# Shifted copies of v made by on-chip DMAs instead of engine copies, in a gated linear attention with a cosine-gated feed-forward layer

## The chip, the core and the metric

One core of one Trainium2 chip runs the whole kernel. The core has a matrix engine (PE in the profile; PEld is its weight load), a vector engine (DVE), an activation engine (ACT), GpSimd (POOL) and a queue engine (SP) that mostly issues DMAs. The metric is the device time of one execution in microseconds (us); lower is better.

## The reference, cut to what matters

```python
f = 1.0 / (1.0 + np.exp(-f_logit))              # q, k, v, f_logit: [4, 8, 768, 48]
for t in range(S):
    state = f[:, :, t, :, None] * state + np.einsum('bhd,bhe->bhde', k[:, :, t], v[:, :, t])
    y[:, :, t] = np.einsum('bhd,bhde->bhe', q[:, :, t], state)
x = y.transpose(0, 2, 1, 3).reshape(3072, 384)  # 8 heads of 48 channels side by side
h = x @ w_in                                    # [3072, 2048]
g = h * np.cos(h)
return (g @ w_out).astype(np.float32)           # [3072, 384]
```

The first part is a linear attention whose 48 x 48 state of each head decays by a gate per channel. It is computed in chunks of 128 tokens: within a chunk by masked scores, between chunks by the state. The second part is a feed-forward layer over all 3072 tokens.

## The kernel before

**Tiling.** The 3072 tokens are 12 pairs of two chunks (three pairs for each of four batch entries). `pair(n)` does the attention for one pair of 256 tokens: it loads f, k, q and v with DMAs (`f{n}`, `k{n}`, ...; pairs 0 and 1 in two halves, `f0.0`, `f0.1`), makes the decays on ACT (`ex`, `ln`, `fx`, then `eb` and `ei` from the cumulated sums `cum` on PE), the decayed q and k (`qa`, `ka`, `qm`, `km` on DVE or POOL), turns those two round (`tq`, `tk` on PE and a copy `qkt`, or for pairs 4 to 11 a DMA transpose `tq` issued on SP), makes the scores (`sc` on PE), masks them (`am` on DVE), carries the state (`ps` on PE, `st` and `sz` on DVE and POOL) and sums the output in PSUM: `y{n}` from masked scores and v, `yi{n}` from the state. `xe{n}.0` and `xe{n}.1` copy it to SBUF as bf16. Of v there is a bf16 cast `vb{n}` and then `vt{n}`, which is the operand that PE loads as weights for `y`.

**The feed-forward part.** `moe(m, ...)` works on units of 128, 128 and then eleven times 256 tokens. `h{m}.js` is the first product (each step 0.65 us of PE in the timeline, 12 matmuls on 128 tokens or 6 on 256), `co` the cosine on ACT, `g` the product on DVE, `o{r}.s` the second product (4 matmuls a step, 0.65 us), `ot` its copy to SBUF and `out` its store. The weights come in eight loads `w0.i` (w_in) and `w1.i` (w_out), each cast to bf16 by `wc`.

**What `vt` is for.** PE writes the output of a head in blocks of 32 of the 384 channels. A head has 48, so blocks 3i and 3i+2 belong to one head and block 3i+1 to two. In the kernel before, `vt` has for each chunk and head 80 columns: 16 zeros, the 48 of v, 16 zeros. `blocks(h)` picks 32 columns at 16 and 48 (even head) or 0 and 32 (odd head), so the shared block gets its half from each head and zeros from the other. Four copies `vt{n}.0` to `vt{n}.3` (64 partitions x 384 each) fill it from `vb`, moving rows between partition halves where the token order asks for it.

**Order.** A string `ORDER` lists every step by hand: its name, its engine (T is PE, S ACT, V DVE, G POOL, Y SP) and the buffer that each new value takes. `emit` issues the steps in this order, so it is the order of each engine's queue; semaphores between the engines follow from what a step reads and writes. A DMA issued on SP waits, on SP, for the data that it reads and for its buffer to be free, and it waits too until the DMA that used its semaphore lane before, eight DMAs earlier, has landed. Steps behind it on the queue wait with it. The steps `zf` are matmuls on zeros at the start.

Of the kernel before, what the change touches and what calls it, by code (L numbers as in the profile page):

```python
# [15 lines left out]
B, H, S, D = 4, 8, 768, 48  # L16
# [13 lines left out]
SLOTS = {"f": 3, "k": 3, "q": 3, "v": 3, "sp": 3, "ls": 2, "b": 3, "bi": 3, "qk": 3, "vb": 3, "vt": 3, "qkt": 5, "am": 4,  # L30
         "sz": 4, "st": 2, "x": 4, "g": 5, "co": 4, "ot": 4}
WITHIN = 12
ZEROS = 38
# [3 lines left out]
f0.0:Y0 f0.1:Y q0.0:S0 f1.1:S1 k0.0:S0 f1.0:Y ex0.0:S q0.1:Y k0.1:Y zsp.0:V zvt.2:V ln0.0:S0 zf0:T0  # L37
zf1:T0 zf2:T0 zf3:T0 zf4:T0 zf5:T0 zf6:T0 zf7:T0 zf8:T0 cum0.0:T0 fx0.0:S ei0.0:S0 ex0.1:S eb0.0:S0
ln0.1:S v0:Y0 ex1.1:S qa0.0:V zqk.2:V ka0.0:G zqk.1:G qm0.0:V2 km0.0:V fx0.1:S qa0.1:V zf9:T1
zf10:T1 zf11:T1 zf12:T1 zf13:T1 zf14:T1 zf15:T1 zf16:T1 tq0.0:T0 cum0.1:T1 ka0.1:G k1.0:Y1 q1.0:Y1  # L40
f2:Y2 k1.1:Y zf17:T2 tk0.0:T ei0.1:S ex1.0:S ln1.0:S0 eb0.1:S qkt0.0:V0 qm0.1:V km0.1:G vb0:V0
zsz.3:G zvt.0:G vt0.1:G2 zsz.2:G zf18:T2 zf19:T2 cum1.0:T2 sc0.0:T0 eb1.0:S1 ln1.1:S tq0.1:T3
cum1.1:T4 tk0.1:T ei1.1:S0 fx1.0:S qkt0.1:S1 am0.0:V0 ka1.0:G zsz.0:V qa1.0:V qm1.0:G1 ei1.0:S
ps0.1:T5,6 ps0.0:T sz0.01:V0 sz0.00:V vt0.0:V km1.0:V q1.1:Y v1:Y1 f3:Y0 vt0.2:S eb1.1:S fx1.1:S
ex2:S ln2:S0 vt0.3:S ka1.1:G zf20:T7 zf21:T7 zf22:T7 zf23:T7 zf24:T7 zf25:T7 zf26:T7 zf27:T7 yi0:T7
tq1.0:T5 tk1.0:T sc0.1:T2 km1.1:G qkt1.0:S1 st0.11:V0 sz0.11:V2 zsz.1:V qa1.1:V st0.10:V am0.1:V1
sz0.10:V vb1:S0 w0.1:Y0 zf28:T0 zf29:T0 zf30:T0 zf31:T0 tk1.1:T6 sc1.0:T4 y0:T2 ex3:S xe0.1:S0
qm1.1:G ln3:S1 am1.0:V2 ad2:G0 tq1.1:T ps1.1:T3,0 ps1.0:T cum2:T1 w0.0:Y1 qkt1.1:V0 st1.00:V0
vt1.2:V2 st1.01:V zf32:T4 sc1.1:T4 ad3:V0 zf33:T6 zf34:T6 zf35:T6 zf36:T6 zf37:T6 cum3:T3 sz1.00:G0
vt1.0:G sz1.01:G vt1.3:G wc0.1:S ei2:S0 ei3:S1 eb2:S0 eb3:S2 w0.2:Y2 am1.1:V0 yi1:T7,6 xe0.0:V  # L50
vt1.1:V w0.3:Y3 h1.01:T4 y1:T st1.10:V0 st1.11:V xe1.0:V1 xe1.1:V h0.01:T0 fx3:S wc0.2:V wc0.0:G
h0.00:T h1.00:T co0.0:S0 co1.0:S1 h2.00:T6 h2.01:T h2.10:T2 h2.11:T g0.0:V2 g1.0:V1 h2.21:T0 h2.20:T
wc0.3:G zsp.1:G co2.0:S2 co2.1:S0 co2.2:S1 h1.10:T4 h1.11:T q3:Y0 w1.0:Y4 k3:Y1 w1.1:Y0 co1.1:S3
g2.0:V3 qa3:V g2.2:V g2.1:V g1.1:V wc1.0:G h0.11:T6 h0.10:T h2.31:T0 qm3.1:V1 co0.1:S1 g0.1:V
h2.30:T ka3:G km3.1:G sz1.10:G0 km3.0:G qm3.0:G wc1.1:S co2.3:S3 g2.3:V sz1.11:V o0.0:T2 q2:Y1
w1.2:Y4 k2:Y0 fx2:S qa2:V ka2:V qm2.1:V2 o1.0:T3 o3.0:T4 o0.1:T o2.0:T5 tk3.0:T6 tq3.0:T tk3.1:T7
o1.1:T tq3.1:T o2.1:T qkt3.0:S0 o3.1:T sc3.0:T0 qkt3.1:S1 w1.3:Y0 v2:Y1 sc3.1:T6 am3.0:V0 wc1.2:G
qm2.0:G km2.0:G km2.1:G o2.2:T o3.2:T am3.1:V2 f4:S2 tq2.0:T0 tk2.1:T1 tq2.1:T wc1.3:G v3:Y0 vb2:S0
qkt2.1:V2 o0.2:T tk2.0:T vt2.0:V2 vt2.1:S ex4:S qkt2.0:V3 ps2.0:T1 ps2.1:T sc2.1:T6 am2.1:V1
st2.01:V0 st2.00:V ln4:S1 o2.3:T o1.2:T o3.3:T sc2.0:T6 vt2.2:G fx4:S ad4:V1 vb3:G1 sz2.00:G2  # L60
vt3.2:V0 ps3.0:T1,0 ps3.1:T f5:Y0 k4:Y0 ot3:S0 ex5:S ln5:S1 o1.3:T cum4:T4 o0.3:T ei4:S0 ot0:S1
ot2:S2 vt3.0:G vt3.1:G sz2.01:G vt2.3:G ka4:G am2.0:V3 vt3.3:V yi2:T6,7 y2:T ot1:V3 sz3.01:V1
sz3.00:V v4:Y1 ad5:V1 xe2.0:V1 q4:Y1 y3:T1,3 yi3:T km4.0:G1 vb4:G1 xe2.1:S eb4:S0 xe3.0:S0 k5:Y1
cum5:T2 v5:Y0 q5:Y0 km4.1:V st3.10:V0 st3.11:V eb5:S1 fx5:S ei5:S0 sz3.11:G1 zsp.2:G sz3.10:V
xe3.1:V h3.11:T6 h3.20:T4 ps4.0:T0,1 ps4.1:T st4.00:V0 st4.01:V qa4:V sz4.00:G0 sz4.01:G st4.10:V0
st4.11:V h3.10:T co3.1:S3 h3.21:T h3.00:T2 h3.01:T co3.2:S1 co3.0:S0 ka5:G km5.1:G2 vb5:G0 qm4.1:G
qm4.0:G zqk.0:G km5.0:G vt4.2:G0 h4.10:T0 h4.11:T g3.1:V2 f7:Y1 f6:Y2 out1:Y co4.1:S3 tq4.1:Y0
# [119 lines left out]
def describe(nc, cpool, ppool, q, k, v, f_logit, moe_w_in, moe_w_out, out):  # L187
    G = Graph()
# [53 lines left out]
    vbS = slots("vb", [128, 2, H, D])  # L242
# [453 lines left out]
```

## Time and profile before

| | before |
|---|---|
| median of 3 runs | 189.81 us (189.21 to 189.86) |
| the profiled execution, its own time | 191.71 us |
| its span, first to last instruction | 189.9 us |
| granted PE clock, mean | 0.980 |
| busy: PE, PEld, DVE, ACT, POOL | 173.3, 124.1, 152.3, 128.5, 95.0 us |
| DMA packets, bytes | 74106, 34.45 MB |
| copies `vt<-vb`: POOL, DVE, ACT | 24 of 552 ns, 12 of 543 ns, 12 of 507 ns (means) |

The profiled execution took 1.8 us more than its span, and 1.9 us more than the median of the runs. A busy PE in the profile is not PE at its peak, since matmuls are pipelined; the number of matmuls by their spacing says more than the busy share. Busy shares over the whole span mix stages: the start up to 25 us, in which little but loading and the first two pairs goes on; a middle up to 150 us, in which pairs and feed-forward units alternate; and a tail in which PE alone works off the second products.

### The profile page before, as it was taken

The page shows a single profiled execution, that of the slowest core. Times are in us where ns is not written, and L with a number is a line of the kernel's source. Part 1 is how long each engine was busy: PE and PEld are TensorE (multiplying, and loading weights), DVE is VectorE, ACT ScalarE, POOL GpSimd, SP SyncE. Part 2 cuts the span into 40 slices and gives each one's busy share as a digit, 9 for nine tenths or more (in the row PEclk, how much of TensorE's full clock was granted, in tenths as well). Part 3 has the DMA queues.
Part 4 walks back from the last instruction along what each step waited for, and adds up shares of the span by engine and source line. Part 5 has one row for each costly group of instructions (what it writes and reads, how often), then busy time and mean ns, then how long its engine had stood idle before and what let it go on. Part 6 is the DMA issues. An engine that isn't in the chain of part 4 may idle for free.

```text
span 189.9 us, 5936 instructions
## 1 busy us (share of the span) xinstructions
PE 173.3 (91%) x2510; PEld 124.1 (65%) x2512; DVE 152.3 (80%) x212; ACT 128.5 (68%) x180; POOL 95.0 (50%) x126
## 2 busy tenths in 40 slices
PE   7779779999979969999999999996989999999992
PEld 2354469855658834778657777665858887666651
DVE  4498999999998998699999899799999898502040
ACT  3959859895579993778795889986634877212321
POOL 2287576838698997446254896499921000000000
PEclk9979999999999996999999999999999999999999
DMA  6999999959996579899799998994790000004043
GB/s 149 261 261 306 387 343 326 289 174 273 265 256 145 147 160 210 194 276 197 195 206 283 268 242 145 232 244 101 102 155 3 3 0 0 3 0 166 0 166 124
DMA packets 74106, 34.45 MB, mean 181 GB/s; under 512 B 67424, under 2 KB 72544, under 8 KB 74080
## 3 DMA queue, kind: packets, MB, share of 16 engines
q1 hardware_dynamic: 70416, 32.71, 72.9%
q10 hardware_dynamic: 3664, 1.38, 3.2%
q8 instruction: 19, 0.31, 0.7%
q14 instruction: 7, 0.06, 0.1%
HBM read 25.17 MB, written 4.72 MB: 157 GB/s over the span
## 4 chain that ended last, share of the span: by engine, by line
PE 35%; DVE 24%; DMA 17%; POOL 7%; ACT 6%; issue 5%; SPq 3%; ACTq 1%; POOLq 0%; DVEq 0%
PE ps L585 18%; DVE g L551 11%; PE ps L569 11%; DMA k<-in_k_dram 7%; DMA v<-in_v_dram 6%; DVE am L448 3%; DVE q L336 3%; POOL qk L394 3%; DMA qkt<-qk 2%; DVE qk L394 2%; DMA out_dram<-ot 2%; PE ps L521 2%; POOL k L344 1%; PE ps L444 1%; SPq L413 1%
## 5 line engine op out<-in xcount | busy, mean ns | idle before, releaser
L574 ACT ACTIVATE co<-ps,halfpi 128x1024 bf16<-128x1024 f32 x48 | 52.0, 1113 | 26.4 <-PE ps L569 25.2
L569 PE MATMUL ps<-x,w_in_bf 128*128 128x256 bf16 (+1 forms) x624 | 67.1, 265 | 2.5 <-DVE g L551 0.9
L585 PE MATMUL ps<-w_out_bf,g 128*128 128x384 bf16 x384 | 69.3, 332 | 0.0
L551 DVE TENSOR_TENSOR g<-ps,co 128x1024 bf16<-128x1024 f32 x48 | 60.1, 1305 | 8.9 <-ACT co L574 8.7
L569 PEld LDWEIGHTS <-w_in_bf 128*128 128x128 bf16 x624 | 56.5, 98 | 11.4 <-issue 3.0
L585 PEld LDWEIGHTS <-g 128*128 128x128 bf16 x384 | 36.5, 99 | 23.0 <-issue 1.3
L448 DVE TENSOR_TENSOR am<-ps,pmask 128x1024 bf16<-128x1024 f32 x24 | 28.8, 1215 | 1.6 <-PE ps L444 1.4
L394 POOL TENSOR_TENSOR qk<-k,bi 128x384 bf16<-128x384 f32 x20 | 21.2, 1068 | 4.2 <-issue 3.3
L493 POOL TENSOR_TENSOR sz<-st,b 64x192 bf16<-64x192 f32 x23 | 13.4, 583 | 17.9 <-DVE st L487 17.0
L394 POOL TENSOR_TENSOR qk<-q,b 128x384 bf16<-128x384 f32 x15 | 15.6, 1049 | 8.2 <-DVE q L336 8.2
L344 POOL TENSOR_TENSOR k<-k,f 128x384 f32<-128x384 f32 (+1 forms) x12 | 11.1, 926 | 7.5 <-DMA k<-in_k_dram 6.3
L195 POOL COPY vt<-vb 64x384 bf16<-64x384 bf16 x24 | 13.2, 552 | 2.0 <-POOL qk L394 0.6
L263 PE MATMUL ps<-zero 128*128 128x512 bf16 x36 | 11.4, 456 | 1.9 <-DVE zero L201 1.2
L195 DVE COPY ot<-ps 128x384 f32<-128x384 f32 x8 | 4.4, 552 | 10.5 <-PE ps L585 10.5
L328 ACT ACTIVATE f<-f 128x768 f32<-128x768 f32 (+1 forms) x14 | 10.4, 746 | 3.6 <-DMA f<-in_f_logit_dram 3.5
L487 DVE TENSOR_TENSOR st<-ps,sz 64x192 f32<-64x192 f32 x32 | 11.2, 352 | 1.6 <-PE ps L521 0.6
L195 ACT COPY ot<-ps 128x384 f32<-128x384 f32 x16 | 7.3, 476 | 6.9 <-PE ps L585 4.8
L444 PE MATMUL ps<-qkt 48*64 48x128 bf16 x384 | 9.0, 220 | 2.8 <-DVE g L551 2.0
L195 ACT CAST x<-ps 128x384 bf16<-128x384 f32 x14 | 6.4, 479 | 6.9 <-DVE x L195 5.1
L336 DVE SCALAR_TENSOR_TENSOR q<-f,q 128x384 f32<-128x384 f32 (+1 forms) x14 | 9.2, 656 | 1.4 <-ACT f L328 1.2
L394 DVE TENSOR_TENSOR qk<-q,b 128x384 bf16<-128x384 f32 x9 | 9.0, 999 | 1.4 <-ACT b L381 1.4
L444 PEld LDWEIGHTS <-qkt 48*64 48x64 bf16 x384 | 6.3, 106 | 5.8 <-issue 3.1
(68 smaller groups left out, 176.3 us busy)
## 6 DMA issues: line engine op xcount, KB each, us to landing
out_dram<-ot SPq DMA_DIRECT2D x24, 192.0 KB, 2.2
v<-in_v_dram SPq DMA_DIRECT2D x11, 384.0 KB, 5.8
q<-in_q_dram SPq DMA_DIRECT2D x10, 384.0 KB, 6.5
k<-in_k_dram SPq DMA_DIRECT2D x10, 384.0 KB, 6.2
f<-in_f_logit_dram SPq DMA_DIRECT2D x9, 384.0 KB, 5.7
g<-in_moe_w_in_dram SPq DMA_DIRECT2D x4, 768.0 KB, 9.3
g<-in_moe_w_out_dram SPq DMA_DIRECT2D x4, 768.0 KB, 7.5
f<-in_f_logit_dram SPq DMA_DIRECT2D x3, 192.0 KB, 4.3
```

The source lines that it names most:

```text
L195: (nc.scalar.copy if e == "ACT" else eng(e).tensor_copy)(out=o, in_=i)
L263: G.step(f"zf{i}", ("PE",), lambda e, dump=dump: nc.tensor.matmul(dump.ap, lhsT=zero[:, 0:128], rhs=zero, start=True, stop=True), writes=[ ...
L336: eng(e).scalar_tensor_tensor(out=w.ap[:, :, 0, :], in0=t.ap[:, :, 1, :], scalar=1.0, in1=w.ap[:, :, 0, :], op0=ALU.add, op1=ALU.mult)
L344: eng(e).tensor_mul(out=w.ap[:, :, 0, :], in0=w.ap[:, :, 0, :], in1=t.ap[:, :, 0, :])
L394: G.step(f"{nm}{n}.{u}", ("POOL", "DVE"), lambda e, u=u, j=j, src=src, dec=dec: eng(e).tensor_mul(out=qkp[u][j].ap[:, :, :, 0:D], in0=swap ...
L444: nc.tensor.matmul(o[t, r, 2 * a + g, :].rearrange("p (e n) -> p e n", e=2), lhsT=qkv(u)[s, 1, a, g, x, :], rhs=qkv(u)[s, 0, a, g, :, :], ...
L448: G.step(f"am{n}.{u}", ("DVE",), lambda e, u=u, sc=sc: nc.vector.tensor_mul(out=am[u].ap.rearrange("p r b n -> p (r b) n"), in0=sc.ap.rear ...
L493: eng(e).tensor_mul(out=new.ap[s, :, r, :].rearrange("p (u a) n -> p u a n", u=2), in0=ap()[s].rearrange("p (u a) n -> p u a n", u=2), in1 ...
L551: nc.vector.tensor_mul(out=o.rearrange("p b (n e) -> p b e n", e=2), in0=ph.ap.rearrange("p (b e n) -> p b e n", e=2, n=64), in1=co.ap.rea ...
L569: nc.tensor.matmul(ph.ap[:, i * T:(i + 1) * T].rearrange("p (g t) -> p g t", t=C), lhsT=w_in_bf[:, kk, f0:f0 + 128], rhs=xa[:, :, kk, :], ...
L574: G.step(f"co{m}.{j}", ("ACT",), lambda e, ph=ph, co=co: nc.scalar.activation(out=co.ap, in_=ph.ap, func=AF.Sin, bias=halfpi), reads=[ph], ...
L585: nc.tensor.matmul(po.ap[:, 0:DM], lhsT=gT.ap[:, j, i * C:(i + 1) * C], rhs=w_out_bf[:, j, :], start=(po.first and j == 4 * s), stop=(po.f ...
```

## The change

The 16 zero columns at each side of `vt` go away: `vt` is now [128, 2, 8, 48] without gaps. The four copies of a pair become four DMAs issued on SP, each of 64 partitions x 768 bytes inside SBUF. A new small tile `vz` holds for each pair of heads 64 columns: the last 16 channels of the even head, 32 zeros, the first 16 of the odd head. One copy of 128 x 256 elements a pair makes it, from `vt`, on DVE, POOL or ACT (2, 6 and 4 of the 12). The shared blocks of `y` read `vz`, the others `vt`. `y{n}` now waits for the four DMAs and for `vz{n}`.

```diff
-SLOTS = {... "vb": 3, "vt": 3, "qkt": 5, ...}
+SLOTS = {... "vb": 3, "vt": 3, "vz": 3, "qkt": 5, ...}
-ZEROS = 38
+ZEROS = 47
...
-    vtS = slots("vt", [128, 2 * H, D + 32], zero=edges)
+    vtS = slots("vt", [128, 2, H, D])
+    vzS = slots("vz", [128, 2, H // 2, 64], zero=lambda t: t[:, :, :, 16:48])
...
         for j, (x, g) in enumerate(((0, 0), (1, 1), (0, 1), (1, 0))):
-            G.step(f"vt{n}.{j}", ("DVE", "POOL", "ACT"), lambda e, x=x, g=g: copy(
-                e, vt.ap[64 * x:64 * x + 64, H * g:H * g + H, 16:16 + D], vb.ap[64 * g:64 * g + 64, x]),
-                reads=[vb], writes=[vtp[j]])
+            G.step(f"vt{n}.{j}", ("SP",), lambda e, x=x, g=g: nc.sync.dma_start(
+                out=vt.ap[64 * x:64 * x + 64, g].rearrange("p h d -> p (h d)"),
+                in_=vb.ap[64 * g:64 * g + 64, x].rearrange("p h d -> p (h d)")), reads=[vb], writes=[vtp[j]])
+        G.step(f"vz{n}", ("DVE", "POOL", "ACT"), lambda e: copy(
+            e, vz.ap.rearrange("p g i (s d) -> p (g i) s d", d=16)[:, :, 0:4:3, :],
+            vt.ap.rearrange("p g (i r) d -> p (g i) (r d)", r=2)[:, :, 32:64].rearrange("p a (s d) -> p a s d", d=16)),
+            reads=[vt], writes=[vz])
...
-            return ((3 * i, 16), (3 * i + 1, 48)) if j == 0 else ((3 * i + 1, 0), (3 * i + 2, 32))
+            return ((3 * i, 0, False), (3 * i + 1, 0, True)) if j == 0 else ((3 * i + 1, 32, True), (3 * i + 2, 16, False))
...
-                   lambda g, b, h, at: dict(lhsT=vt.ap[:, H * g + h, at:at + 32],
-                                            rhs=am[h // 4].ap[:, h % 2, h % 4 // 2 * 2 + g, :]))
+                   lambda g, b, h, at, z: dict(
+                       lhsT=vz.ap[:, g, h // 2, at:at + 32] if z else vt.ap[:, g, h, at:at + 32],
+                       rhs=am[h // 4].ap[:, h % 2, h % 4 // 2 * 2 + g, :]))
...
-        G.step(f"y{n}", ("PE",), inner, reads=[am[0], am[1], vt], writes=py, sums=True)
+        G.step(f"y{n}", ("PE",), inner, reads=[am[0], am[1], vt, vz], writes=py, sums=True)
```

`ORDER` is a new list throughout, with other engines for some steps. Counted over the list: DVE loses 12 `vt`, 2 `qm`, 1 `km`, 1 `vb`, 3 `ad` and 2 `xe` and gains 2 `vz` and 1 `ot`; ACT loses 12 `vt`, 1 `wc` and 1 `ot` and gains 4 `vz`, 2 `xe` and 1 `qkt`, and issues 6 loads where it issued 5; POOL loses 24 `vt` and gains 6 `vz`, 3 `ad`, 2 `qm`, 1 `km`, 1 `vb` and 1 `wc`. SP issues 144 DMAs where it issued 96. ACT still changes between its two tables ten times. Nine more zero matmuls stand at the start.

The head of SP's and ACT's queues, which set the start (buffer numbers left out):

```
SP before:  f0.0 f0.1 f1.0 q0.1 k0.1 v0 k1.0 q1.0 f2 k1.1 q1.1 v1 f3 w0.1 w0.0 w0.2 w0.3 q3 w1.0 k3 ...
SP after:   f0.1 f1.0 q0.0 k0.1 f1.1 k0.0 q0.1 v0 q1.1 k1.1 q1.0 f3 k1.0 vt0.2 vt0.1 vt0.0 k3 vt0.3
            vt1.3 vt1.2 f2 vt1.0 w0.3 vt1.1 w0.2 w0.0 w0.1 w1.3 w1.2 q2 k2 w1.0 v2 v3 w1.1 f5 vt2.3 f4 vt3.0 vt2.0 vt2.1 ...
ACT after:  f0.0 ex0.0 ln0.0 ex0.1 ex1.0 fx0.0 ln0.1 fx0.1 ei0.1 eb0.0 ln1.0 ex1.1 ei0.0 ln1.1 eb0.1 fx1.1 eb1.1 eb1.0
            qkt0.0 ei1.0 ei1.1 fx1.0 v1 ex3 ln3 q3 vb1 fx3 qkt1.1 eb3 ei3 qkt1.0 vz0 ex2 ln2 xe0.1 vz1 ...
PE before its first h1.01: all of pairs 0 and 1 but y1 (it stands one place later), cum2, cum3
PE after before its first h0.11: all of pairs 0 and 1, cum2, cum3, tk3.x, tq3.x, sc3.1
```

More of the change, by code (lines that the diff above doesn't have):

```diff
@@ L38 @@
[L38 to L49, printed above, removed]
@@ L56 @@
[L56 to L67, printed above, removed]
@@ new lines @@
+zf0:T0 zf1:T0 zf2:T0 zf3:T0 zf4:T0 zf5:T0 zf6:T0 zf7:T0 zf8:T0 cum0.0:T0 fx0.1:S k0.1:Y0 f1.1:Y
+k0.0:Y q0.1:Y zf9:T1 zf10:T1 zf11:T1 zf12:T1 zf13:T1 cum0.1:T1 qa0.0:V ka0.0:V zqk.0:G zsz.0:G
+ei0.1:S0 eb0.0:S0 ln1.0:S1 ka0.1:G zsp.0:G km0.1:G1 ex1.1:S ei0.0:S ln1.1:S km0.0:G zsz.2:G eb0.1:S
+fx1.1:S qm0.0:V qa0.1:V qm0.1:V v0:Y0 q1.1:Y1 k1.1:Y1 zf14:T2 zf15:T2 zf16:T2 zf17:T2 zf18:T2
+cum1.0:T2 zf19:T3 zf20:T3 zf21:T3 cum1.1:T3 tk0.1:T1 zf22:T4 tk0.0:T0 tq0.0:T vb0:G0 zf23:T4 zf24:T4
+zf25:T4 zf26:T4 ps0.0:T4,5 tq0.1:T ps0.1:T eb1.1:S1 eb1.0:S qkt0.0:S0 ei1.0:S0 ei1.1:S fx1.0:S
@@ new lines @@
+ka1.1:V qa1.1:V q1.0:Y f3:Y2 k1.0:Y zvz.2:V sz0.01:V2 qa1.0:V v1:S0 km1.1:G1 ex3:S qm1.0:G ka1.0:G
+km1.0:G zsp.2:V sz0.00:V qm1.1:V qkt0.1:V1 ln3:S0 sc0.0:T2 zf27:T6 zf28:T6 zf29:T6 zf30:T6 zf31:T6
+tk1.1:T0 zf32:T6 zf33:T6 zf34:T6 zf35:T6 zf36:T6 zf37:T6 zf38:T6 sc0.1:T6 yi0:T1 tq1.0:T4 st0.11:V0
+st0.10:V vt0.2:Y0 vt0.1:Y vt0.0:Y k3:Y0 q3:S1 vt0.3:Y am0.1:V0 ad3:G2 vb1:S1 fx3:S sz0.10:G2 zf39:T5
+tk1.0:T tq1.1:T ka3:G ps1.1:T5,6 ps1.0:T cum3:T7 qkt1.1:S0 eb3:S2 ei3:S0 qkt1.0:S1 sz0.11:V
+st1.00:V0 st1.01:V am0.0:V1 sc1.1:T2 qa3:V vz0:S2 km3.1:G1 qm3.0:G km3.0:G sc1.0:T4 vt1.3:Y1 vt1.2:Y
@@ new lines @@
+f2:Y1 ex2:S am1.1:V2 qm3.1:V am1.0:V3 y0:T7 tk3.1:T0 sz1.00:G0 sz1.01:G tq3.0:T2 zf40:T3 zf41:T3
+zf42:T3 tk3.0:T tq3.1:T qkt3.1:V2 zf43:T3 zf44:T3 yi1:T3,4 ln2:S0 xe0.1:S0 vt1.0:Y w0.3:Y0 vt1.1:Y
+vz1:S2 zf45:T5 zf46:T5 y1:T sc3.1:T0 qkt3.0:S0 xe0.0:S st1.10:V0 ad2:V2 st1.11:V cum2:T5 wc0.3:G
+ei2:S0 eb2:S0 fx2:S xe1.0:V1 sz1.10:V0 xe1.1:V w0.2:Y1 w0.0:Y2 h0.11:T6 h1.11:T2 wc0.2:G h2.30:T4
+am3.1:V2 w0.1:Y3 h1.10:T co1.1:S0 wc0.0:V g1.1:V2 w1.3:Y4 h2.31:T h0.10:T h2.21:T0 h2.20:T wc0.1:G
+sz1.11:G co0.1:S1 wc1.3:G h2.01:T2 h2.00:T g0.1:V1 h2.11:T6 h2.10:T co2.2:S0 g2.2:V3 w1.2:Y0 q2:Y1
@@ new lines @@
+k2:Y0 h0.01:T0 h0.00:T co2.3:S2 co2.0:S1 w1.0:Y4 v2:Y0 wc1.2:G v3:Y1 co2.1:S0 g2.3:V g2.0:V zvz.0:V
+g2.1:V ka2:G qa2:V qm2.0:G0 qm2.1:G h1.00:T4 h1.01:T co1.0:S1 co0.0:S0 o2.3:T2 o2.2:T o1.3:T3
+o0.2:T6 o3.3:T7 o0.3:T o1.2:T wc1.0:S w1.1:Y0 km2.0:G zsz.3:V g0.0:V km2.1:V g1.0:V tq2.1:T0 o2.0:T
+tk2.1:T vb2:S1 ps2.0:T1 ps2.1:T vb3:G0 tk2.0:T4 tq2.0:T o0.0:T o1.0:T st2.00:V0 st2.01:V qkt2.1:V1
+qkt2.0:S3 ps3.1:T4,5 ps3.0:T sc2.0:T0 sz3.00:V3 am2.0:V3 sz3.01:V f5:Y2 sz2.00:G2 wc1.1:G st3.10:V1
+st3.11:V vt2.3:Y1 o3.0:T o3.2:T f4:Y1 o3.1:T ex5:S o1.1:T ln5:S0 sc3.0:T4 sc2.1:T0 ot1:V0 ad5:G2
@@ new lines @@
+sz2.01:G am3.0:V0 am2.1:V1 vt3.0:Y0 vt2.0:Y vt2.1:Y vt2.2:Y vt3.2:Y k4:Y0 ex4:S o0.1:T o2.1:T
+cum5:T3 yi2:T4,5 ln4:S1 ot0:S1 vz2:S0 fx4:S ad4:G1 eb5:S0 ei5:S0 cum4:T6 ei4:S1 y2:T ka4:G km4.1:G1
+vt3.3:Y vt3.1:Y vz3:V2 ot3:V2 v4:Y1 xe2.0:V0 vb4:G0 f7:Y0 y3:T3,0 yi3:T km4.0:V ot2:V3 sz3.10:V3
+xe3.1:V1 xe2.1:S eb4:S1 fx5:S xe3.0:S ex7:S h3.01:T4 h3.10:T6 ps4.1:T2,3 ps4.0:T h3.00:T sz3.11:G
+st4.00:V1 st4.01:V sz4.00:G0 h3.20:T0 h3.11:T h3.21:T co3.0:S1 q4:Y1 co3.1:S0 sz4.01:G qa4:V
+st4.11:V1 st4.10:V k5:Y1 out3:Y vt4.2:Y0 q5:Y0 qm4.0:G qm4.1:G ka5:G km5.1:G0 km5.0:G out0:Y vt4.1:Y
@@ L526, in inner @@
         def inner(e):
[L527 to L529 removed]
+            summed([(g, b, h, at, z) for g in range(2) for h in range(H) for b, at, z in blocks(h)],
+                   lambda g, b, h, at, z: dict(
+                       lhsT=vz.ap[:, g, h // 2, at:at + 32] if z else vt.ap[:, g, h, at:at + 32],
+                       rhs=am[h // 4].ap[:, h % 2, h % 4 // 2 * 2 + g, :]))
         def inter(e):
```

109 lines of the change are left out of this document (51 added, 58 removed).

## The prediction

> **What bounds the kernel now.** I read the page first (busy time, slices), then the table by stage, the waits of PE in the middle, and the timeline round the longest of them.
>
> ```profile
> PE 173.3 (91%) x2510; PEld 124.1 (65%) x2512; DVE 152.3 (80%) x212; ACT 128.5 (68%) x180; POOL 95.0 (50%) x126
> PE   7779779999979969999999999996989999999992
> DVE  4498999999998998699999899799999898502040
> PEclk9979999999999996999999999999999999999999
> ```
>
> PE and DVE stand at nine tenths together up to slice 32; then DVE runs out and PE goes on alone to the end. The granted clock is below full in two slices only: the third, and the sixteenth (71 to 76 us).
>
> ```profile
> 30.00:60.00 30.00, 28.09 (x468) 20.82 (x466) 29.08 (x40) 23.08 (x30) 21.52 (x25) 1.00 1.05 256
> 60.00:90.00 30.00, 28.01 (x411) 21.05 (x409) 27.26 (x34) 23.82 (x32) 21.44 (x28) 0.94 0.93 187
> 90.00:120.00 30.00, 29.07 (x454) 21.14 (x453) 27.69 (x34) 24.98 (x33) 18.31 (x23) 1.00 1.00 222
> 120.00:150.00 30.00, 27.64 (x540) 20.79 (x539) 28.35 (x41) 20.17 (x31) 17.33 (x23) 1.00 0.60 124
> ```
>
> The columns are the stretch, its length, busy time of PE, PEld, DVE, ACT and POOL, clock, DMA share, GB/s. From 30 to 150 us PE stands idle for 1.9 + 2.0 + 0.9 + 2.4 = 7.2 us, and DVE is busy for 112.4 of 120. So PE is the bound, and DVE, nearly as full, sets most of what PE still loses:
>
> ```profile
> PE ps L444 <- DVE g L551: 2.0, 1, 2.0
> PE ps L521 <- DVE am L448: 1.4, 1, 1.4
> ```
>
> ```profile
> 68.44 1.72 DVE L195 COPY vt<-vb 64x384 bf16<-64x384 bf16 x1
> 70.20 2.51 DVE L551 TENSOR_TENSOR g<-ps,co 128x1024 bf16<-128x1024 f32 x2
> 71.56 0.42 PE L444 MATMUL ps<-qkt 48*64 48x128 bf16 x16 [1.99 <-DVE g L551]
> 71.91 4.34 PE L585 MATMUL ps<-w_out_bf,g 128*128 128x384 bf16 x16
> ```
>
> One `vt` copy on DVE took 1.72 us at 68.44 (the median of these is 0.256). Behind it `g` came late, PE stood for 1.99 us, and its next 16 second-product matmuls took 4.34 us where 16 took 2.76 at 66.46 us, in the slice with the low clock. That one copy is the visible head of a loss of 2.0 + 1.6 = 3.6 us.
>
> **The change part by part.** What goes:
>
> ```profile
> L195 POOL COPY vt<-vb x24: 493/502/847, 12.3 to 142.8; 64x384 bf16<-64x384 bf16 x24
> L195 ACT COPY vt<-vb x12: 495/508/512, 14.2 to 145.1; 64x384 bf16<-64x384 bf16 x12
> L195 DVE COPY vt<-vb x12: 241/256/1724, 14.4 to 122.7; 64x384 bf16<-64x384 bf16 x12
> ```
>
> That is 13.2 us of POOL, 6.1 of ACT and 6.5 of DVE. The `vz` copies put back 128 x 256 elements each; no row is that, and between 0.26 (the `vt` median on DVE) and 0.55 (a `vt` on POOL) I take 0.5 on POOL, 0.3 elsewhere: 3.0, 1.2 and 0.6 us. With the steps that change engine, at the row means, DVE falls by about 12 us in all (6.5 - 0.6 of v; 2 `qm` 2.0, `km` 0.7, `vb` 0.7, 3 `ad` 1.9, 2 `xe` 1.1; `ot` +0.6), ACT by 4, POOL by 2. PE's work stays, but for nine zero matmuls that fill waits of the start.
>
> *The start* (before: first h at 25.22 us). In the new order PE may begin with h only behind `cum2`, so behind f2, and f2 stands on SP behind two `vt1` copies, which wait for `vb1`. On ACT: f0 lands at 4.16 as now; up to `v1` stand eight steps `ex` and `ln` of 0.52, four `fx` of 0.36, eight `ei` and `eb` of 0.33 and `qkt0.0`, 1.01: 13.4. v1 lands 4.6 later (the row of v on ACT's queue), 18.0; `vb1` 0.83: 18.85. Two copies at 0.4 each on SP, then f2 at 19.65 (landing 5.7): 25.35. `ex2`, `ln2` 0.83 + 0.84, `ad2` 0.63, `cum2` 0.56: first h at 28.2, so 3.0 later. By then PE has done 1.6 us more of other work (`y1`, pair 3's four transposes and one score step: 7.8 us against 6.2 at the spacing of the timeline). Net **+1.4 us**; with f2 landing in 3.4 (the shortest of a load) it is -0.9, with the weights late it is +5.0 (a rival below).
>
> *Pairs 2 and 3* (before: 41.4 to 56.8 us). PE had 11 o steps (7.2 us) and attention steps of 5.5 to do in 15.4 us and lost 2.7. In the new order pair 3's transposes and one score are already made, so only pair 2 is still to be turned. Against that, `vt2.0` to `vt2.2` stand on SP behind `vt3.0`, and so behind `vb3` on POOL. I take half of the loss back: **-1.3**, between 0 and -2.7.
>
> *The middle.* Nine of the twelve DVE copies stand after 30 us, 4.6 us of them, with the one of 1.72 among them. Without it the stall at 69.6 goes: **-3.6**. What comes late next is am (1.4 us of PE once), which I leave, since the room that DVE gains may go to any wait: 0, at best -1.2.
>
> *What the DMAs cost.* SP issues 48 more.
>
> ```profile
> out_dram<-ot SPq DMA_DIRECT2D x24, 192.0 KB, 2.2
> v<-in_v_dram SPq DMA_DIRECT2D x11, 384.0 KB, 5.8
> qkt<-qk SPq DMA_TRANSPOSE x16, 3.4
> L592 SPq DMA_DIRECT2D out_dram<-ot x24: 332/450/1473, 60.6 to 187.1; - x24
> ```
>
> The last column of the first three is issue to landing in us; the last row has the time that an issue holds SP, in ns. A copy of 48 KB in 64 rows is nearest to the store: 0.33 to 0.53, I take 0.4, and it lands in about 2.2 us on an empty queue, up to 5.8 behind a load. From 60.1 to 122.4 us SP issues 44 DMAs for 46.35 us and is free for 15.95; 24 copies (pairs 4 to 9) add 9.6, so 56 of 62. In the packets, 48 x 64 = 3072 more are 4% of 74106. `vb` to `y` grows from one engine copy to issue, landing and `vz`: 0.4 x 4 + 2.2 + 0.5 = 4.3 us at the least. From pair 4 on a run of h or o steps of that length lies between in PE's order. Cover is thin where SP is held by a producer: I take three waits of PE of 0.5 us (the wait for `DMA qkt<-qk` of the profile), **+1.5**; ends 0 and 6.4 (rival).
>
> Sum: 1.4 - 1.3 - 3.6 + 1.5 = -2.0; the span goes from 189.9 to 187.9. The profiled execution (191.71 in all) would be 189.7; the runs' median lies 0.1 below its span, so **187.8 us**.
>
> **The rivals.** *SP becomes the bound.* Each `vt` waits on SP for `vb`, and loads, stores and transposes stand behind it. If SP's free 15.95 us are waits for producers that stay, the 9.6 us make it late from 60 us on. For: at 101.47 a load of v was issued whose landing (4.77 us) is in the chain that ended last, so there was no lead; transposes hold SP for 1.2 to 2.7 us each. Against: other loads lie long before their use. It decides once SP is later than the lead of the loads. With two thirds of 9.6 reaching PE, 6.4 in place of 1.5: **192.7**. Slower.
>
> *The copies land one behind another.* Four landings of 2.2 in a row are 8.8 us, 5.0 more than the 3.8 above (four issues and one landing). It would show where the plan has least cover, at pairs 2 and 3, whose copies stand together on SP while PE has only o steps left, and decide if those run out first: 5.0 on top, **192.8**. Slower. For: DMA share is 1.0 or more in most stretches to 120 us. Against: stores queued closely in the tail do not add up so. The Trainium skill ("DMA: Bandwidth & Descriptors", Rules for kernel authors) speaks against the change here: it says to coalesce small transfers, since under 64 KB one pays mostly overhead, and that two transfers to halves of the partitions serialize. By its fit of about 2.0 us + bytes / 436 GB/s a copy would be an estimated 2.1 us, near the row of the store.
>
> *The weights come late.* `w0.3` is issued at 21 here (the first w_in load before: 13.36). If it takes the median of 9.3, it lands at 30.3; the cast, 1.46, lets h begin at 31.8, 3.6 after my sum: **191.4**. Slower. Against: the 9.3 is of four queued together.
>
> *Nothing gained.* DVE's 12 us are off the path, the stall comes back under another name at another place (again with a lowered clock), and the rest of the sum stays: 189.8 + 1.4 - 1.3 = **189.9**, no change.
>
> **How the numbers follow.** No change means within 0.5% (0.95 us), about what a measurement of this kernel can tell. The forecast has 0.46, all faster; nothing gained 0.13; SP 0.20, landing 0.10, weights 0.11, together 0.41 slower. The forecast's own range is 184.0 (f2 early, pairs 2 and 3 without loss, no new wait gives 189.8 - 0.9 - 2.7 - 3.6 = 182.6, not all at once) to 188.8. The range of 8 in 10 reaches up over the rivals to 194.0, since the SP case may be larger than its two thirds.
>
> **What would show it.** Right: no wait of PE over 1.5 us between 30 and 150 us, full clock there, DVE's busy time near 140 us, first h near 28 us, `vt` landing in 2 to 4 us. Wrong: PE or DVE waiting for `DMA vt<-vb` or for `vz`; SP issuing without a gap from 60 to 125 us, with POOL and ACT waiting for loads of k, q and v; the first h after 30 us.

## The result and the profile after

The changed kernel took 197.9 us (median of 196.9, 197.9 and 198.3), the kernel before beside it 189.8: a ratio of 1.040 (from all runs kept, not from the two medians), interval 1.030 to 1.050. It is slower; the forecast was 187.8 with a range up to 194.0. Here and below, medians and ratios leave out runs more than 1.5% above the fastest of their kernel, as one of the change at a clock of 0.57 and 292 us. SP issues 144 DMAs in the new order; in the old one it was 97, one more than stated above.

The page of the profiled execution after the change (197.9 us in all, span 196.1): busy time by engine, two engines by slices, the granted clock by slices.

```profile
PE 176.2 (90%) x2521; PEld 125.7 (64%) x2521; DVE 143.0 (73%) x193; ACT 123.6 (63%) x173; POOL 92.1 (47%) x116
PE   7899499999959998998896999997999799999991
DVE  5399987997966996897993599787999589721020
PEclk9999889999999999999996999999999999999999
```

DVE lost 9 us of work (12 were costed), ACT 5 and POOL 3, and DVE now has slices of 3, 5 and 6 in the middle. PE did not get shorter for it. After the start there is again one slice with a low clock, now the twenty-second (103 to 108 us) instead of the sixteenth.

The table by stage (stretch, length, busy time of PE, PEld, DVE, ACT, POOL, clock, DMA share, GB/s):

```profile
30.00:60.00 30.00, 27.25 (x431) 20.70 (x429) 24.98 (x32) 22.26 (x29) 19.25 (x19) 1.00 1.04 280
60.00:90.00 30.00, 28.88 (x436) 23.01 (x434) 24.31 (x30) 25.53 (x32) 20.63 (x26) 1.00 1.10 221
90.00:120.00 30.00, 26.45 (x396) 19.24 (x395) 23.96 (x32) 20.71 (x28) 15.18 (x19) 0.94 0.95 199
120.00:150.00 30.00, 28.38 (x540) 19.82 (x539) 25.43 (x34) 19.90 (x31) 17.69 (x24) 1.00 0.89 188
```

PE is idle for 9.0 us of these 120, against 7.2 before. The stretch from 90 to 120 lost 2.6 us of busy time, more than the stretch from 60 to 90 gained. DVE has over 4.5 us free in every stretch, though PE still waited twice for its `g` (below).

The longest waits, first of PE, then of the other engines for what the change added (total, times, longest, in us):

```profile
PE ps L449 <- DMA qkt<-qk: 2.1, 1, 2.1
PE ps L591 <- DVE g L557: 2.0, 2, 1.1
PE ps L449 <- DVE am L453: 1.9, 1, 1.9
PE ps L526 <- POOL vz L196: 1.7, 2, 1.3
PE ps L526 <- DMA vt<-vb: 0.7, 1, 0.7
PE ps L526 <- DVE vz L196: 0.7, 1, 0.7
```

```profile
POOL vz L196 <- DMA vt<-vb: 10.9, 3, 6.4
DVE vz L196 <- DMA vt<-vb: 1.8, 1, 1.8
```

The first wait is for a transpose, not for a copy; the one for `am` lies in the start, at 19.6 us; three are for the copies and their tails (`vz`), 3.1 us together, 1.3 of them behind the middle, at 152 us; and POOL stood 10.9 us with `vz` at its head, with everything behind it in its order standing too. The timeline round the first wait (start, length, engine, step; idle before it in brackets):

```profile
94.14 2.93 SPq L418 DMA_TRANSPOSE qkt<-qk  x2
97.13 0.57 SPq L598 DMA_DIRECT2D out_dram<-ot  x1
97.76 1.11 SPq L404 DMA_DIRECT2D vt<-vb  x2
98.92 1.32 SPq L418 DMA_TRANSPOSE qkt<-qk  x1
104.61 0.50 PE L449 MATMUL ps<-qkt 48*64 48x128 bf16 x16 [2.10 <-DMA qkt<-qk]
105.05 1.46 PE L591 MATMUL ps<-w_out_bf,g 128*128 128x384 bf16 x4
```

SP issues the third transpose behind a store and two copies, though its data were ready on POOL at about 92.7. It lands 5.65 us after its issue at 98.92, and PE has run dry. The next four second-product matmuls take 1.46 us where four took 0.81 at 101.70; the granted clock from 100 to 110 us is 0.83. Before, the stall of 1.99 had the same tail: 0.83 from 69.5 to 79.5 us. The page's rows for the DMAs and the rows of the new steps (ns: shortest, median, longest; first and last start in us):

```profile
vt<-vb SPq DMA_DIRECT2D x48, 48.0 KB, 3.5
L404 SPq DMA_DIRECT2D vt<-vb x48: 462/588/2152, 12.1 to 151.0; - x48
DMA to landing us min/median/max: 1.8/3.5/6.4
L196 POOL COPY vz<-vt x6: 388/400/403, 70.5 to 153.1; 128x256 bf16<-128x256 bf16 x6
```

By place: the first h starts at 29.31 (before 25.22), the h of unit 3 at 58.97 (56.80), the last matmul ends at 191.8 (186.6), and after it come 4.3 us (3.3). The two spans differ by 6.2 us; the medians of the runs by 8.1, since the profiled execution of before was 1.9 above its own median.

### The profile page after: what moved, and what is told of

The parts are those of the page before. It is cut to its first block, busy times and chain, and to the rows that moved or that the text cites. A ratio compares the mean times of both kernels' runs of the same rounds, so it can differ in the third digit from the quotient of the medians.

```text
span 196.1 us, 6001 instructions
## 1 busy us (share of the span) xinstructions
PE 176.2 (90%) x2521; PEld 125.7 (64%) x2521; DVE 143.0 (73%) x193; ACT 123.6 (63%) x173; POOL 92.1 (47%) x116
## 4 chain that ended last, share of the span: by engine, by line
PE 48%; DMA 27%; DVE 7%; SPq 6%; POOL 4%; ACT 3%; issue 2%; POOLq 0%; DVEq 0%; ACTq 0%
PE ps L591 23%; PE ps L575 20%; DMA k<-in_k_dram 8%; DMA f<-in_f_logit_dram 6%; DMA qkt<-qk 5%; DMA g<-in_moe_w_in_dram 5%; DVE g L557 3%; POOL qk L395 3%; SPq L404 3%; DMA out_dram<-ot 2%; PE ps L526 2%; SPq L296 2%; PE ps L449 1%; DVE am L453 1%; PE ps L471 1%
## 5 line engine op out<-in xcount | busy, mean ns | idle before, releaser
L591 PE MATMUL ps<-w_out_bf,g 128*128 128x384 bf16 x384 | 67.5, 328 | 2.0 <-DVE g L557 2.0
L395 POOL TENSOR_TENSOR qk<-k,bi 128x384 bf16<-128x384 f32 x21 | 22.2, 1069 | 2.2 <-ACT f L341 1.5
L196 ACT COPY ot<-ps 128x384 f32<-128x384 f32 x15 | 6.8, 480 | 25.7 <-PE ps L591 23.7
L395 POOL TENSOR_TENSOR qk<-q,b 128x384 bf16<-128x384 f32 x17 | 17.2, 1023 | 4.4 <-DVE q L337 4.3
L264 PE MATMUL ps<-zero 128*128 128x512 bf16 x47 | 14.7, 444 | 1.2 <-DVE zero L202 1.2
L337 DVE SCALAR_TENSOR_TENSOR q<-f,q 128x384 f32<-128x384 f32 (+1 forms) x14 | 10.3, 733 | 4.5 <-POOL k L345 2.1
L354 POOL TENSOR_TENSOR sp<-ls 128x384 bf16<-128x384 f32 x8 | 7.9, 999 | 9.6 <-ACT ls L333 7.6
L196 ACT CAST x<-ps 128x384 bf16<-128x384 f32 x16 | 7.2, 480 | 8.3 <-PE ps L526 5.1
L526 PE MATMUL ps<-am,vz 128*32 128x128 bf16 x192 | 7.8, 230 | 2.4 <-POOL vz L196 1.7
```

Source lines behind the costliest of these rows:

```text
L196: (nc.scalar.copy if e == "ACT" else eng(e).tensor_copy)(out=o, in_=i)
L264: G.step(f"zf{i}", ("PE",), lambda e, dump=dump: nc.tensor.matmul(dump.ap, lhsT=zero[:, 0:128], rhs=zero, start=True, stop=True), writes=[ ...
L395: G.step(f"{nm}{n}.{u}", ("POOL", "DVE"), lambda e, u=u, j=j, src=src, dec=dec: eng(e).tensor_mul(out=qkp[u][j].ap[:, :, :, 0:D], in0=swap ...
L526: nc.tensor.matmul(py[g].ap[32 * c:32 * c + 32, C * m:C * m + C], start=(py[g].first and (g, c) not in begun), stop=(py[g].final and left[ ...
L591: nc.tensor.matmul(po.ap[:, 0:DM], lhsT=gT.ap[:, j, i * C:(i + 1) * C], rhs=w_out_bf[:, j, :], start=(po.first and j == 4 * s), stop=(po.f ...
```

## The experiments

The theory after the result: SP issues everything in one order, and 48 more issues, each with a landing behind it, make transposes, loads and copies late. Rivals: the bytes in the DMA engines; SP's wait for `vb` with work queued behind it; the new order itself, whatever it carries; and one bad place (the transpose at 98.92).

**Neither order with its copies.** The prediction's two halves, taken apart. `vt` holds zeros and nothing is copied, in the old order and in the new one:

```diff
-            G.step(f"vt{n}.{j}", ..., lambda e, x=x, g=g: <the copy>, reads=[vb], writes=[vtp[j]])
+            G.step(f"vt{n}.{j}", ..., lambda e: None, reads=[vb], writes=[vtp[j]])
```

> The kernel before with its four copies of a pair left out (y reads zeros, PE's work is the same): the most that any way of taking the copies off the engines could bring in that order. The prediction's step (the copy of 1.72 us on DVE heads a loss of 3.6, DVE gets 4.6 us of room) says 185.5 to 187. If the copies lie off the path, 189 to 190.

> The new order with vt and vz left out altogether: y reads tiles that hold zeros (so the attention within a chunk is left out of the result, PE's work is the same). If the copies and the waits for them are what the change costs, about 190 (198 less the 8). If the order does, 195 or more. With the run that has engine copies it splits the price: the difference to the full change is all that DMA copies and vz cost in this order.

Old order without copies: 187.5 us, ratio 0.984 (0.978 to 0.990). New order without copies: 189.5 us, 0.995 (0.991 to 0.999). So taking the copies off the engines is worth 1.6% (3.0 us), and the order alone is 1.1% (2.1 us) worse than the old one: with free copies it would have come out near where the old kernel stands. The granted clock in the profiled run of the first was full throughout:

```profile
PEclk9999999999999999999999999999999999999999
```

**The copies issued, but read by nobody.** `y` takes a constant tile in place of `vt` and `vz`; `vz` is not made; all 48 DMAs run.

```diff
-                       lhsT=vz.ap[...] if z else vt.ap[:, g, h, at:at + 32],
+                       lhsT=zt[:, g, h, (16 if z else at):(16 if z else at) + 32],
-        G.step(f"y{n}", ("PE",), inner, reads=[am[0], am[1], vt, vz], ...)
+        G.step(f"y{n}", ("PE",), inner, reads=[am[0], am[1]], ...)
```

> The full change, its 48 DMAs on SP with their waits for vb, but nothing waits for them: vz is left out and y reads a constant tile of zeros (the attention within a chunk is left out of the result). Against the new order without copies (189.5) this shows what the DMAs cost by holding SP alone. If SP's queue is the cause, 195 to 198. If it is the landing and vz ahead of y, 190 to 191.

194.7 us, ratio 1.020 (1.010 to 1.030), and PE still waits for a transpose:

```profile
PE ps L449 <- DMA qkt<-qk: 2.4, 1, 2.4
```

About half of the DMAs' price (2.5 of 4.5 points, each uncertain by about one) is there though no step needs them. The rest of the way to 1.040, about 2.0% or 3.7 us, comes with the reading: waits for landings and for `vz`, and SP's waits until `vt`'s buffers are free again. These were not taken apart.

**Bytes or number.** Three edits of that kernel: the same 48 DMAs with 32 bytes a row instead of 768; two DMAs a pair of 128 rows (the same bytes); two of the four DMAs of 64 rows a pair (the two that cross rows).

```diff
-                out=vt.ap[64 * x:64 * x + 64, g].rearrange(...), in_=vb.ap[64 * g:64 * g + 64, x].rearrange(...)
+                out=vt.ap[64 * x:64 * x + 64, g, 0, 0:16], in_=vb.ap[64 * g:64 * g + 64, x, 0, 0:16]   # 48 small
+                out=vt.ap[:, g].rearrange(...), in_=vb.ap[:, x].rearrange(...)) if x == g else None      # 24 of 128 rows
+                <as before>) if x != g else None                                                         # 24 of 64 rows
```

> The order of the changed kernel, the copies made for the products by nobody, and 48 DMAs on SP that nothing reads, of 64 rows of 32 bytes each instead of 768: the shifted copies of v are left out of the result. With the same 48 DMAs at 768 bytes a row the ratio was 1.020 (about 194.4 us where the kernel before takes 190.6), without any 189.5. If the price of the unread copies is their number, that is the time that each holds SP's queue ahead of transposes and loads, the time stays at 193.5 to 195.5 us. If it is the bytes that they move beside the loads, it falls to 189 to 191 us.

> As the run with 48 unread DMAs of 768 bytes a row, but two DMAs of 128 rows a pair in place of four of 64 rows: 24 DMAs, the same bytes; the shifted copies of v are again left out of the result. If the price goes by the number of DMAs, half of the 5 us between 189.5 and 194.4 is left, about 192 us. If it goes by the bytes, the time stays at 193.5 to 195.5 us.

> The order of the changed kernel with only the two crossing DMAs of a pair, 24 of 64 rows of 768 bytes, which nothing reads (the shifted copies of v are left out of the result). Two DMAs of 128 rows a pair gave 188.8 us, four of 64 rows 194.4. If the number is what costs, 188.5 to 190.5 us; if it is DMAs of 64 rows as such, about 192 us.

48 small ones: 193.8 us, 1.017 (1.009 to 1.025), not to be told from the 1.020 of the large ones, with 4% of their bytes. 24 of 128 rows: 187.9 us, 0.986 (0.979 to 0.994). 24 of 64 rows: 189.1 us, 0.989 (0.984 to 0.995). So it is the number, not the bytes and not the shape; nor the place of any one copy, since the two runs with 24 keep different ones (`vt.0` and `vt.1` of each pair, or `vt.2` and `vt.3`). The first 24 cost nothing that shows: these runs even lie a little below the 0.995 without any, so up to a point between two such kernels need not be the copies' doing. The second 24 cost 3 points, about 6 us. Nor did the other DMAs become slower: on the two pages the transposes land in 3.4 us in the median before and after, the stores in 2.2 and 2.1. The rows of SP's issues in the timeline between 30 and 150 us add up to 78.0 us with no copies, 87.3 and 89.2 with 24, and 99.5, 101.1 and 100.6 with 48 (small, large, the change itself), of 120. SP is never full. But an order in which each entry waits for the one ahead and for its own producer runs late before it is full; that the time on SP is what the number stands for fits all six sums, and is argued, not isolated. It can hold for this order only: the old order with the DMAs (below) has 87.4 us of them and costs far more.

**SP's wait for `vb`.** The DMAs of the change copy a constant tile, so that none waits for `vb`; `vz` and `y` still wait for their landing (`y`'s products are of that constant).

```diff
-                in_=vb.ap[64 * g:64 * g + 64, x].rearrange("p h d -> p (h d)")), reads=[vb], writes=[vtp[j]])
+                in_=zt[64 * g:64 * g + 64, x].rearrange("p h d -> p (h d)")), writes=[vtp[j]])
```

> The full change, but the 48 DMAs read a constant tile of zeros, so they do not wait on SP for the cast vb (v is left out of y within a chunk); y and vz wait for them as before. If what costs is that SP stands still for vb with loads and transposes behind, this falls to 191 to 193. If it is the issue time and the landing, it stays at 196 to 198.

199.2 us, 1.041 (1.033 to 1.050): nothing is won back. SP's wait for `vb` is not the price. As `y` multiplies zeros here too, the zeros of the runs without copies are not what makes those fast.

**One bad place: the transpose ahead of the copies, the loads ahead of the copies.** Only words of ORDER move.

```diff
-... tq7.0:Y3 tq7.1:Y0 out2:Y vt7.1:Y vt6.2:Y tq6.0:Y2 ...
+... tq7.0:Y3 tq7.1:Y0 tq6.0:Y2 out2:Y vt7.1:Y vt6.2:Y ...
```

> The full change with one transpose (tq6.0) issued on SP ahead of out2, vt7.1 and vt6.2 in place of behind them. In the trace of the change it was issued 6 us after its data was there, landed after 5.65, and PE waited 2.1 us for it, then ran 10 us at a clock of 0.83. If SP's queue makes that wait, it goes, and the time falls by 1.5 to 3.5 us, to 195 or 196. If the transfer would have been late anyway, no change.

Its four runs took 195.8 to 199.9 us; the ratio is 1.031 (1.019 to 1.043), an interval that holds the change's own 1.040. The wait for the transpose is gone from PE's list, and in its place:

```profile
PE ps L526 <- POOL vz L196: 1.9, 3, 1.2
PE ps L526 <- DMA vt<-vb: 1.9, 2, 1.1
```

Those were 1.7 and 0.7: at least part of the loss changed its name. In the other run, f2 and the four loads of w_in go ahead of the copies of pair 1 (words `f2`, `w0.3`, `w0.2`, `w0.0`, `w0.1` before `vt1.3`).

> The full change with the loads f2, w0.3, w0.2, w0.0 and w0.1 issued on SP ahead of pair 1's copies, which stand for vb1. In the trace f2 was issued at 19.2 and w0.0 landed at 32.0, where DVE stood for it. If the start is late because these copies hold the loads back, the first h comes at 27 or before and the time falls by 1 to 2.5 us. If DVE's own work makes the start late (as without copies, where the first h came at 30.9), the first h stays at 28.5 or later and the time within 1 us.

203.6 us, 1.066 (1.059 to 1.073), worse, which neither theory had. The copies of pair 1, issued from 21.5 to 23.9 us, land 9.4 to 10.5 us after their issue, behind the loads; `y1` waits in PE's order, and the first h behind it moves from 29.31 to 35.24:

```profile
PE ps L526 <- DMA vt<-vb: 5.6, 1, 5.6
```

Here a DMA was not only issued late behind others, it also landed late behind them.

**Copies of each kind in the other order.** The new order with engine copies in the places of the DMAs (on the engines that the old order names), and the old order with the DMAs right behind `vb` and `vz` ten words before `y`.

```diff
-            G.step(f"vt{n}.{j}", ("SP",), lambda e, x=x, g=g: nc.sync.dma_start(...))
+            G.step(f"vt{n}.{j}", ("DVE", "POOL", "ACT"), lambda e, x=x, g=g: copy(...))      # new order
```

> The new order, the new vt and vz, but the four copies of a pair made by DVE, POOL and ACT (as the kernel before assigned them) in place of DMAs on SP. If the DMA copies cost the time (SP's queue and the landing of the copies), this falls to 191 or below, from 198. If the new order itself is slower, whoever makes the copies, it stays at 195 or above. In between, both have a part, in proportion.

> The order of before, 38 zero matmuls, but vt by four DMAs on SP, issued right behind the cast vb of the pair (or behind the y that frees the buffer), and one small vz copy some ten steps ahead of y. If the DMA copies cost the time, 195 or more. If the new order does, 188 to 191, with DVE's 4.6 us after 30 us freed.

Engine copies in the new order: runs between 196.3 and 203.9 us, too far apart for a ratio. DMAs in the old order: 224.0 us, 1.177 (1.170 to 1.184), with PE waiting for the transposes at eight places:

```profile
PE ps L448 <- DMA qkt<-qk: 14.6, 8, 6.3
```

The second shows what the new order is for: it pays 2 us so that the same DMAs, placed with room, cost 8.4 in place of some 36 (1.177 against 0.984). The first shows little: an engine copy in a place made for a DMA holds its whole engine, and in its trace one copy on DVE took 3.87 us (28.99 to 32.86), while three casts ran on POOL.

**Half of the issues on ACT's queue.** The last two DMAs of each pair are issued by ACT at the same place of the order.

```diff
-            G.step(f"vt{n}.{j}", ("SP",), lambda e, x=x, g=g: nc.sync.dma_start(
+            G.step(f"vt{n}.{j}", ("SP", "ACT"), lambda e, x=x, g=g: eng(e).dma_start(
```

> The order of the changed kernel with all 48 DMAs, but the last two of each pair issued by ScalarE at the same place in the order. If it is the hold of SP's queue that costs, about half of the 5 us comes back: 193 to 196 us against 198.1. If ScalarE's own steps now wait behind its issues and behind the cast of v, 198 us or more.

213.7 us, 1.118 (1.111 to 1.125). ACT has to stand at the issue until `vb` is there, with its own chain behind it (argued from the order), and the copies that it issues land in 4.4 us in the median, those of SP in 2.7:

```profile
PE ps L526 <- DMA vt<-vb: 10.1, 3, 5.2
```

So this run can't say what SP would gain; it says that a second queue is no free place when its engine has work.

**Half of the copies back on engines.** What the counts point to: the two copies a pair that stay on their own rows are made by an engine right ahead of `vz` (the engine of `vz`, or ACT always), the two that cross rows stay DMAs, 24 in all.

```diff
+            if x == g:
+                G.step(f"vt{n}.{j}", ("DVE", "POOL", "ACT"), lambda e, x=x, g=g: copy(
+                    e, vt.ap[64 * x:64 * x + 64, g], vb.ap[64 * g:64 * g + 64, x]), reads=[vb], writes=[vtp[j]])
+                continue
```

> The order of the changed kernel; of the four copies of a pair the two that stay on their own rows go back to an engine, the one that makes the tails, right ahead of the tails; only the two that cross rows stay DMAs on SP: 24 DMAs. Without anything reading them, 24 DMAs gave 188.8 us, 48 gave 194.4, and reading added about 3.7. If the number of DMAs in SP's order is the larger part of the price, 5 us are won back and the two engine copies cost about 1: 190 to 194 us against 198.1. If it is the wait for the landing that counts, 195 us or more, since two still have to land.

> As the run with half of the copies back on the engines, but all 24 engine copies on ScalarE (about 0.5 us each, 12 us in all) instead of the engine that makes the tails. By the number of DMAs 190 to 194 us, as there; if the place of the engine copies decides, that is if ScalarE's other steps come late behind them, 2 us or more above that run.

195.7 us, 1.023 (1.017 to 1.028), and with all on ACT 198.6 us, 1.040 (1.034 to 1.047). The first is clearly better than the change, and at the upper edge of the 190 to 194 that was expected of the number alone (1.023 of 189.8 is 194.1). Between the two runs only the engine of the 24 copies differs, and it is worth 1.8 points. PE no longer waits long for a transpose (0.8 us), but still for the tails; POOL again stands for a landing:

```profile
PE ps L530 <- POOL vz L195: 2.2, 3, 0.9
POOL vz L195 <- DMA vt<-vb: 4.6, 1, 4.6
```

Against the 0.989 of the same 24 DMAs unread, 3.3 points (6 us) are the price of two landings, `vz` and 24 engine copies together; which of them it is was not tried.

**What the old order's stall was.** The prediction's largest term rests on one copy of 1.72 us. In the old order that copy alone goes to ACT (`vt5.3`), or all nine DVE copies from pair 2 on do.

```diff
-... vt5.3:V ...
+... vt5.3:S ...      # in the second run also the other eight
```

> The kernel before in its own order with one edit: the one copy of v that takes 1.72 us on VectorE at 68.44 us goes to ScalarE. The prediction put a loss of 3.6 us (a stall of 1.99 and the slow clock behind it, 1.6) to that copy. If it heads that loss and nothing else comes late, about 187 us. If the stall only moves on to the next late step, 190 to 191 us, no different from the kernel before at 190.7.

> The kernel before in its own order with all nine VectorE copies of v from the third pair on moved to ScalarE, where such a copy takes about 0.51 us. Without any copies that order took 187.5 us, which is the bound here. If it is room on VectorE that taking copies away brought, 187.5 to 189.5 us. If it is the work itself, on whatever engine, or if ScalarE's own steps come late instead, 190.5 us or more.

189.9 us, 0.996 (0.991 to 1.000), and 191.4 us, 1.002 (0.998 to 1.006). Moving the one copy wins 0.9 us (1.7 at the end of the interval), not 3.6; giving DVE the room of nine wins nothing. In the first of them the stall at 69.6 us is gone, as predicted, but one of the same size stands at 75.9 to 78.1 us with the same slow clock (0.83 from 75 to 85), and its head is not a copy (timeline, as above):

```profile
76.38 0.56 DVE L194 CAST vb<-v 128x768 bf16<-128x768 f32 x1 [2.71 <-DMA v<-in_v_dram]
76.86 1.22 DVE L447 TENSOR_TENSOR am<-ps,pmask 128x1024 bf16<-128x1024 f32 x1
78.13 0.42 PE L443 MATMUL ps<-qkt 48*64 48x128 bf16 x16 [2.23 <-DVE am L447]
```

DVE stands idle for 2.71 us for a load of v, then casts it, and `am`, queued behind, reaches PE 2.23 us late. So a load on SP's queue was the next late step in the old order as well. No kernel that computes with the copies came out clearly ahead of the kernel before; only kernels whose `y` leaves v out did.

Why that one copy took 1.72 us can be read in the traces. It began while POOL worked on two `qk` products (68.10 to 70.06) and ended just behind them. Of the twelve DVE copies before, the five over 0.4 us all began while an instruction ran on POOL; with POOL idle a copy took 0.25. In the change the two `vz` copies on DVE took 0.78 us beside POOL and 0.20 without. So most of the 1.72 looks like a wait and not work; no run moved POOL's work to show it.

## Why the prediction was wrong, point by point

The runs divide the change of +4.0% into four steps, each the difference of two ratios, so each uncertain by about half a point to one and a half:

| step | from the runs | points | us of 190 | predicted |
|---|---|---|---|---|
| copies off the engines, old order | 1 to 0.984 | -1.6 | -3.0 | -3.6 |
| new order, still without copies | 0.984 to 0.995 | +1.1 | +2.1 | +0.1 (1.4 - 1.3) |
| 48 DMAs that nobody reads | 0.995 to 1.020 | +2.5 | +4.7 | together |
| their being read: landings, buffers, `vz` | 1.020 to 1.040 | +2.0 | +3.7 | +1.5 |

*The middle, -3.6.* The size is about right for the removal of all 48 copies (-3.0), by luck, since the reason is not. The step "that one copy is the visible head of a loss" failed: with that copy on ACT its stall went, but only 0.9 us came back, because a stall behind a late load took its place. What brings the 3.0 us when all copies go stays open. In the changed kernel even that gain is not to be seen: a wait for a transpose stands there, with the same slow clock behind it. The 3.6 was also read off a long execution, 1.9 us above the median: of the 54 runs of the kernel before beside the experiments, 13 had a mean granted clock of 0.982 or less, like this one (0.980), the others 0.987 or more. So most had less slow clock to win back.

*The start, +1.4.* `vb1` started at 17.15 (18.0 predicted) and f2 was issued at 19.22 (19.65): that chain held. The first h came at 29.31 instead of 28.2, behind the weights and `cum2`, and the h of unit 3 was 2.2 us late where 0.1 was forecast. In the trace without copies it is late by 1.0, in those with 24 unread ones not at all (56.65 and 56.30 against 56.80), in those with 48 unread ones it comes at 56.19 (small) and 57.91. So about half of the 2.2 or more came with the reading of the copies, not with the start.

*Pairs 2 and 3, -1.3.* In the trace of the change PE waits there for `vt` (0.7) and for `vz` on DVE (0.7), which itself stood 1.8 us for a landing. The gain was eaten in place.

*The DMAs, +1.5.* This is the term that failed: 8.4 us (4.7 + 3.7), beyond its upper end of 6.4. The step that failed most is that the cost was set by SP's free time, as if an in-order queue costs nothing until it is full. Between 60 and 125 us SP's issues fill 53.6 of 65 us, and it was late all the same. Two sizes were too small besides. A landing takes 3.5 us in the median, up to 6.4, not 2.2: the median of the store, 11 of whose 24 stand in a tail with an empty queue, was taken for the middle, where DMA share is about 1. The trace of before had it: its 13 stores between 60 and 141 us landed in 3.7 us in the median. And an issue holds SP for 0.59 us, not 0.4, and up to 2.15; but this decided nothing, since in the prediction's own stretch (60.1 to 122.4 us) SP's issues took 51 us, fewer than the 56 that it had added up. The rule of the Trainium skill that the prediction weighed ("DMA: Bandwidth & Descriptors", Rules for kernel authors: coalesce small transfers) points the right way, for a price per transfer; the runs with 32 bytes a row (1.017) and with half as many DMAs (0.986 and 0.989) bear it out. Its 2.1 us of a copy by the fit, which the page gives for DMAs that GpSimd issues, is near the shortest landing here (1.8) and well under the 3.5 of the median in this traffic.

*The rivals.* "SP becomes the bound" names the right queue and the right sign at 192.7, but the wait for `vb` that it begins with was not the reason (1.041 without it), and SP kept its gaps. "The copies land one behind another" (192.8) has the right place and not the right reason: four copies of pairs 2 and 3, issued from 47.08 to 49.59 us, landed 5.1 to 3.5 us after their issue, so within a microsecond of one another; each landing was long, they did not add up. The two price different things, issuing and landing, and were weighed as if only one could come. Their sum on top of the forecast, 187.8 + 4.9 + 5.0, would have been 197.7; that it meets the 197.9 is partly luck, as other terms were off too. The mechanism of "nothing gained", the stall back under another name with a lowered clock, is what the traces show up to 104.6 us in the change and up to 78.1 us with the one copy on ACT.

*What would show it.* Of the signs of failure, waits for `DMA vt<-vb` and `vz` came (10.9 us on POOL); SP without a gap did not, and the first h stayed under 30. Two signs of success did not come: PE had a wait over 1.5 us (2.1), and the clock was not full (0.94 from 90 to 120 us). DVE at 143 us and the landing at 3.5 stood among the signs of success and were met in a kernel that is 4% slower: they say that the work moved, not that it paid.

## What to carry to other kernels

Price a DMA that takes the place of an engine copy by its number in the issuing queue, with its landing at the traffic of the stage where it falls, and with what stands behind it in that queue; a queue with a sixth of its time free was already late in this planned order. Where two rivals price different things, add them before setting the range. A stall's nearest neighbour on the engine is a suspect: move that one instruction alone, and see how much comes back, before a whole change is costed by it; and look at what ran on the other engines while it was slow.

## What had not been expected of the hardware

24 more small DMAs on SP cost nothing that shows, in this order; 48 cost 3 points more than these, and the bytes (32 or 768 a row) made no difference. On the price of issuing, the Trainium skill, "DMA: Bandwidth & Descriptors" (Issuing engines are not separate DMA queues), says that the sequencer's time to start a DMA "is usually small relative to the DMA itself". One by one the trace does not contradict it (0.59 us against a landing of 3.5), but the issues add up on one queue: the new DMAs raise SP's issue time between 30 and 150 us from 78 to 101 us.

A bf16 copy of 64 x 384 on DVE took up to seven times as long when it began beside work on POOL (0.45 to 1.72 us against 0.25 with POOL idle).

A stall of PE of about 2 us was followed by a lower granted clock, before (1.99 us, then 0.94 from 60 to 90 us) and after (2.10 us, then 0.83 from 100 to 110 us). The Trainium skill, "TensorE: Matmul & The Clock Gate" (HAM oscillation), gives the rule "no PE-idle gaps >~3.4µs"; in these two traces shorter gaps stood ahead of a slower clock. Nor does a gap of this size decide it alone: in the run with 48 small copies PE stood for 2.3 us up to 103.9 us, and the clock was full from 100 to 110; in the run with the transpose moved ahead it was 0.50 from 57.6 to 61.0 us, with no single gap over 0.9 us in the 7 us ahead, but with PE busy for only 2.6 of the last 4.0. What the gap alone did was not tried apart from what led up to it.
